# Pooled attention and two feed-forward networks: the start of the kernel is put in another order

## The chip, the core and the metric

The kernel runs on one core of a Trainium2 chip. The metric is the device time of one execution in microseconds (us), taken as the median of several runs. Five engines work side by side: TensorE (PE, with its weight loads PEld), VectorE (DVE), ScalarE (ACT), GpSimd (POOL) and SyncE (SP), whose queue (SPq) issues the transfers (DMAs). Each engine runs its own list of instructions strictly in order.

## What is computed

```
k_p, v_p = mean of k, v over groups of 8 rows             # 8 images, 8 heads, 576 x 64 each
attn = softmax(q @ k_p.T / 8)                             # 576 x 72 for each head
x    = concat over heads of attn @ v_p                    # 4608 tokens x 512
y    = leaky_relu(x @ w_in) @ w_out                       # 512 -> 2048 -> 512
out  = (silu(n @ w_gate) * (n @ w_val)) @ w_out2          # n = RMS norm of y; 512 -> 1536 -> 512
```

All in float32. The kernel makes each large product from two parts of a number, a high part (fp32r) and a low part (the rest), as three matmuls.

## The kernel before

**Stages.** First comes the attention of image 0, then the first network over nine tiles of 512 tokens (j = 0 to 8) with the attention of the other images in between, then the second network. The change lies in the start: the attention of image 0 and the conversion of w_in and w_out, which arrive raw and have to be turned into high and low parts before TensorE can use them.

**Attention of image 0** is a list of steps, named by kind: `kp` (k summed over 8 rows, one DVE reduction of a 128x512 tile, L239), `kt` (k transposed on PE, copied by ACT to kblk, L295), `t` (q transposed), `vp` (`v_prep`, L248), `s` (scores on PE at L325; on DVE maxima L331, subtraction L332; the exponential on ACT L336; on DVE sums L337, L338, reciprocal L339, multiplication L340), `x` (exponentials transposed on PE at L369 and L374, split into parts by ACT and DVE, L371 to L379), `av` (the product with v on PE at L395 and L400, split to the tile `xhl` that the first network reads). Tokens 0 to 255 of the image are the query tiles t = 0, 1 and end in four `av0` steps; the rest, t = 2 to 4 and four `av1` steps, is a list of 13 steps called `second`.

`v_prep` works on six tiles of v: r = 0 to 3 of 128 rows, r = 4 and 5 the "rest" of 96 rows. For image 0 the sum over 8 rows is one DVE reduction (L254); for later images it is `pool_sum` (two additions on GpSimd, L229) and a third addition (L259). Then GpSimd multiplies by a mask (`vm`, L263), ACT takes the high part and DVE the low part (L95, or L270 and L272 for the rest).

**Weights.** `Weights` (W1) holds a list of 36 pieces: w_in and w_out blocks in turn (i0, o0, i1, o1, ...), 28 of them whole (512 KB) and the last 8 in halves. `load` asks for one; `begin` is two instructions on the raw piece, an ACT activation (L139, shown as L98) and a DVE tensor_scalar (L141); `end` is a DVE scalar_tensor_tensor (L149), the high part on ACT and the low part on GpSimd or DVE in turn (both at L95 and L92 in the trace). `step` ends the piece begun, asks for more, and begins the next.

**What sets the order.** The program is traced in the order of the Python code, and a planner with its own model of time then orders each engine's instructions: it may put one that it thinks ready ahead of those traced before it. `tc.keep_in_program_order(x)` ties x behind the instruction traced last before it on its engine, in issue order only. The traced order is `before` (L430 to L443: kp, kt, t, then s0, s1, the six vp, x0, x1, four av0), with one `W1.step` after s1 and one after x1 (L583). Then tile j = 0 runs 24 jobs: f = 0 to 7 on tokens 0 to 255, f = 8 to 15 on all 512, and f = 0 to 7 on tokens 256 to 511. A job f has a `h_unit` (needs w_in block f and xhl), attention slots (the 13 steps of `second` are spread over the first 15 slots, two in a job), the `y_unit` of two jobs earlier (needs w_out of that block and the low part of the activation, DVE L605), and two `W1.step`, three from f = 11 on. The job f = 8 reads all of xhl, so it needs all of `second`.

The transfers of image 0 are asked for in one list (L565 to L574): k, q0, q1, v r = 0 to 4, then i0 and o0, v r = 5 and q2, then i1 and o1, q3, q4, the gain, and four more pieces of weights.

Of the kernel before, what the change touches and what calls it, by code (L numbers as in the profile page):

```python
# [8 lines left out]
F32 = mybir.dt.float32  # L9
# [13 lines left out]
def pooled_attention_then_two_ffns(  # L23
# [13 lines left out]
    nc = tc.nc  # L37
    B, H, S, D = q.shape
    NT, DM = out.shape
    P = 128  # L40
    POOL = 8
    SP = S // POOL
    NP = H // 2
# [45 lines left out]
    def split(hi_eng, hi, lo_eng, lo, src):  # L89

        if hi_eng is nc.scalar:
            nc.scalar.activation(out=hi, in_=src, func=AF.Copy)  # L92
        else:
            hi_eng.tensor_copy(out=hi, in_=src)
        lo_eng.tensor_tensor(out=lo, in0=src, in1=hi.bitcast(F32), op=ALU.subtract)  # L95

    def prelu(out, in_, alpha, scale=1.0):
        return nc.scalar.activation(out=out, in_=in_, func=AF.Prelu, scale=scale, alpha=alpha)  # L98
# [8 lines left out]
    class Weights:  # L107
# [25 lines left out]
        def begin(self):  # L133
            x = self.loaded.pop(0)
            t = x[2]
            top, low = t[:, :, 1], t[:, :, 0]


            prelu(top.bitcast(F32), top.bitcast(F32), 2.0 ** 32, scale=2.0 ** -112)  # L139

            nc.vector.tensor_scalar(  # L141
                out=low, in0=low.bitcast(U32), scalar1=0.9374 * 2.0 ** -29, scalar2=None, op0=ALU.mult
            )
            self.begun.append(x)

        def end(self):
# [22 lines left out]
    ap = att.__enter__()  # L169
# [55 lines left out]
    def pool_sum(x):  # L225

        n = POOL * D // 2
        while n >= 2 * D:
            nc.gpsimd.tensor_tensor(out=x[:, :n], in0=x[:, :n], in1=x[:, n:2 * n], op=ALU.add)  # L229
            n //= 2  # L230
# [17 lines left out]
    def v_prep(b, r):  # L248
        rest = r >= NP
        n = R3 if rest else P  # L250
        x = vraw.pop((b, r))[0:n]
        vs = ap.tile([P, D], F32, tag="vs", bufs=2, name=f"vs{b}_{r}")[0:n]
        if b == 0:
            nc.vector.tensor_reduce(  # L254
                out=vs, in_=x.rearrange("p (r d) -> p d r", r=POOL), axis=AX.X, op=ALU.add
            )
        else:
            pool_sum(x)
            nc.gpsimd.tensor_tensor(out=vs, in0=x[:, 0:D], in1=x[:, D:2 * D], op=ALU.add)  # L259
        m = mask_rest.rearrange("p q h -> p (q h)") if rest else mask_main  # L260
        c = m.shape[1]
        vm = ap.tile([P, 4, D], F32, tag="vm", bufs=1, name=f"vm{b}_{r}")[0:n, 0:c]
        nc.gpsimd.tensor_tensor(  # L263
            out=vm, in0=vs.unsqueeze(1).to_broadcast([n, c, D]),
            in1=m.unsqueeze(2).to_broadcast([n, c, D]), op=ALU.mult,
        )
        if rest:

            t = ap.tile([R3, 4, D], F32R, tag="vbr", bufs=2, name=f"vb{b}_{r}")
            nc.scalar.activation(out=t, in_=vm, func=AF.Copy)  # L270
            z = slice(2 * R1, 3 * R1)
            nc.vector.tensor_tensor(out=t[z], in0=vm[z], in1=t[z].bitcast(F32), op=ALU.subtract)  # L272
        else:
            t = ap.tile([P, 2, 2, D], F32R, tag="vb", bufs=4, name=f"vb{b}_{r}")
            split(nc.scalar, t[:, HI], nc.vector, t[:, LO], vm)
        vb[b, r] = t
# [144 lines left out]
    def need(kind, b, t):  # L421
        if b < B and (kind, b, t) not in done:
            done.add((kind, b, t))
            seq.append((kind, b, t))
# [5 lines left out]
    for part, rs in enumerate(((0, 1, 2), (3, 4))):  # L430
        for r in rs:
            need("kp", 0, r)
        need("kt", 0, part)
        need("t", 0, part)
    need("s", 0, 0)
    need("s", 0, 1)
    for r in range(NP + 2):
        need("vp", 0, r)
    need("x", 0, 0)
    need("x", 0, 1)  # L440
# [9 lines left out]
    for i, (b, t) in enumerate(tiles):  # L450
# [20 lines left out]

    emit = {
        "kp": k_prep, "vp": v_prep, "kt": step_kt, "t": step_t, "s": step_s,
        "x": step_x, "av0": lambda b, p: step_av(b, 0, p), "av1": lambda b, p: step_av(b, 1, p),
    }
# [54 lines left out]
    def run_step(x):  # L530
        kind, b, t = x
        if b > 0:
            top_up(1 if W1.left() else 3)
        emit[kind](b, t)
        if b > 0 and kind in use:
            live["q" if kind == "t" else "kv"] -= 1
# [25 lines left out]
    W1 = Weights(todo1, lambda x: (8 if x[0][1] < 6 else 4) if x[1].stop - x[1].start == 512 else 2)  # L562
# [3 lines left out]
    first += [("q", 0, t) for t in range(2)] + [("v", 0, r) for r in range(NP + 2)]  # L566
    first += [("q", 0, t) for t in range(2, 5)]
    for i in range(0, len(first), 2):
        if i in (12, 14):
            W1.load()  # L570
            W1.load()
        t = per.tile([P, 2, 512], F32, tag=f"w{24 + i // 2}", bufs=1, name=f"first{i}")
        for z, (kind, b, r) in enumerate(first[i:i + 2]):
            {"q": load_q, "k": load_k, "v": load_v}[kind](b, r, t[:, z, :])  # L574
# [5 lines left out]
        W1.load()  # L580
    for x in before:
        run_step(x)
        if x[0] in "sx" and x[2] > 0:  # L583
            W1.step()

    gp = {}
# [95 lines left out]
    def side_steps():  # L682
# [28 lines left out]
        def at(step, f):  # L711
            steps.setdefault(step, []).append(f)

        def unit(begin, n, name, out, src, srcs_of, zs):


# [22 lines left out]
            def store(i):  # L739
                for x, d, dst in held[i]:  # L740
                    own(nc.sync.dma_start(out=dst, in_=d.bitcast(F32).rearrange("p a h n -> p a (h n)")))

            at(begin, start)
            at(begin + 5, lambda: convert(held["raw"]))
            if len(zs) == 2:
# [9 lines left out]
        for p in range(NPAIR):  # L755
            for m, src in (("g", w_gate), ("v", w_val)):
                for c in range(2):
                    def srcs(raw, m=m, p=p, c=c):
                        x = raw.bitcast(F32).rearrange("p (k i n) w -> p k i n w", k=2, i=2)
                        y = op_dram[m, p]  # L760
                        return (
                            ((x[:, 0, :, :, 0], y[:, 1, :, c, :]), (x[:, 1, :, :, 0], y[:, 2, :, c, :])),
                            ((x[:, :, 0, :, 1], y[:, 0, :, c, :]), (x[:, 1, 1:2, :, 1], y[:, 3, 0:1, c, :])),
                        )

                    unit(
                        begin, n, f"{m}{p}_{c}", lambda t: t.rearrange("p (k f) w -> p k (f w)", k=2),
                        src[:, p * 2 * W:(p + 1) * 2 * W].rearrange("(k c p) f -> c p k f", k=2, p=P)[c], srcs,
                        ((0, 6), (1, 8)),
                    )  # L770
                    begin += 6
                    n += 1
            for f in (2 * p, 2 * p + 1):
                def srcs(raw, f=f):
                    x = raw.bitcast(F32)[:, :, 1].unsqueeze(1)
                    return (((x, wo_dram[f].rearrange("p h n -> p (h n)").unsqueeze(1)),),)

                unit(
                    begin, n, f"p{f}", lambda t: t.rearrange("p n w -> p (n w)"), rows(w_out2, f), srcs,
                    ((f % 2, 7),),  # L780
                )
                begin += 4
                n += 1
# [478 lines left out]
```

## Time and profile before

| what | us |
|---|---|
| median of 3 runs | 1807.55 (1806.89 to 1810.25) |
| the profiled execution | 1812.26 |
| its span, first to last instruction | 1810.50 |
| PE busy | 1758.0 |
| DVE, ACT, POOL busy | 891.1, 670.4, 551.2 |

The profile is of one execution. "Busy" counts an engine's instructions; where an engine waits, the row gives the idle time before the instruction in brackets and what released it. PEclk is the granted TensorE clock, where 1.00 is 2.4 GHz and 0.50 is 1.2 GHz. PE is busy nearly all of the span; the time in which it isn't lies mostly in the first 130 us.

### The profile page before, as it was taken

To read this page: it belongs to the slowest core of one execution; us is meant where nothing else is said; L and a number is where in the kernel's file an instruction comes from. 1 tells how busy PE (TensorE), PEld (TensorE's weight loads), DVE (VectorE), ACT (ScalarE), POOL (GpSimd) and SP (SyncE) were. 2 spreads that over 40 slices of the span, in tenths; PEclk is the share of its full clock that TensorE was granted. 3 is DMA by queue.
4 is the path that set the end of the run, shared out by engine and by line. 5 is a ranking of instruction groups with operands and counts; after the bars stand their busy time and mean duration, and the time that the engine had idled before them with its cause. 6 is when DMAs were issued, how large, how long until landed. Compare 5 with 4: busy or idle time off the path is not lost.

```text
span 1810.5 us, 23634 instructions
## 1 busy us (share of the span) xinstructions
PE 1758.0 (97%) x8596; PEld 1498.0 (83%) x8596; DVE 891.1 (49%) x1603; ACT 670.4 (37%) x1424; POOL 551.2 (30%) x681
## 2 busy tenths in 40 slices
PE   3899999999999999999999999999999999999999
PEld 2889887878888888888888888899788889978887
DVE  7974435454356555455344345345534444553331
ACT  5754333443344444344343332243232323322220
POOL 2653303334125142211110442154144204413320
PEclk6999999999999999999999999999999999999999
DMA  8833204447365555435451766687775668776562
GB/s 253 307 109 89 55 21 143 157 140 230 101 189 157 163 157 162 145 125 180 157 172 45 234 195 211 228 300 245 255 245 196 193 226 314 245 250 224 186 209 93
DMA packets 175555, 330.81 MB, mean 183 GB/s; under 512 B 54352, under 2 KB 90192, under 8 KB 174928
## 3 DMA queue, kind: packets, MB, share of 16 engines
q1 hardware_dynamic: 175440, 329.31, 56.1%
q8 instruction: 68, 1.11, 0.3%
q14 instruction: 47, 0.39, 0.1%
HBM read 277.87 MB, written 51.38 MB: 182 GB/s over the span
## 4 chain that ended last, share of the span: by engine, by line
PE 89%; DVE 5%; DMA 3%; issue 1%; ACT 1%; SPq 1%; POOL 1%; ACTq 0%; DVEq 0%; POOLq 0%
PE y L628 20%; PE h L592 20%; PE o L1089 16%; PE yg L1014 6%; PE yv L1014 6%; PE xv L1014 4%; PE xg L1014 4%; PE wg L1014 4%; PE wv L1014 4%; PE sc L325 2%; PE av L395 1%; PE xt L369 1%; DMA wo<-wo 1%; PE qt L303 1%; DMA y<-ye 1%
## 5 line engine op out<-in xcount | busy, mean ns | idle before, releaser
L592 PE MATMUL h<-xhl,w_i 128*128 128x512 f32 (+1 forms) x1824 | 438.2, 385 | 3.1 <-ACT xhl L92 1.3
L592 PEld LDWEIGHTS h<-xhl,w_i 128*128 128x128 f32 x1824 | 329.5, 191 | 68.3 <-DVE xhl L95 4.1
L1089 PE MATMUL o<-wo,u 128*128 128x512 f32 x1296 | 315.1, 390 | 3.5 <-DMA wo<-wo 3.4
L628 PE MATMUL y<-ghl,w_o 128*128 128x512 f32 (+1 forms) x1296 | 285.1, 365 | 1.4 <-DVE ghl L605 1.4
L1089 PEld LDWEIGHTS o<-wo,u 128*128 128x128 f32 x1296 | 242.0, 188 | 53.0 <-DMA wo<-wo 4.9
L628 PEld LDWEIGHTS y<-ghl,w_o 128*128 128x128 f32 x1296 | 218.9, 191 | 35.1 <-DVE ghl L605 1.8
L605 DVE TENSOR_TENSOR ghl<-g,ghl 128x512 fp32r<-128x512 f32 (+1 forms) x152 | 114.6, 754 | 241.5 <-ACT g L98 238.3
L98 ACT ACTIVATE ghl<-h 128x512 fp32r<-128x512 f32 (+1 forms) x152 | 87.0, 572 | 233.4 <-PE h L592 232.9
L628 PE MATMUL y<-ghl,wr 128*128 128x512 f32 x624 | 158.9, 395 | 0.0
L628 PEld LDWEIGHTS y<-ghl,wr 128*128 128x128 f32 x624 | 115.1, 188 | 22.4
L95 POOL TENSOR_TENSOR u<-e2g,u 128x512 fp32r<-128x512 f32 (+1 forms) x25 | 29.7, 1190 | 308.3 <-ACT u L92 308.3
L229 POOL TENSOR_TENSOR v<-v 128x256 f32<-128x256 f32 (+2 forms) x84 | 59.7, 713 | 107.6 <-DMA v<-in_v_dram 105.0
L98 ACT ACTIVATE g<-h 128x512 f32<-128x512 f32 (+1 forms) x152 | 86.8, 571 | 1.0 <-DVE ghl L605 1.0
L1014 PE MATMUL yg<-T,ag 128*128 128x512 f32 (+1 forms) x360 | 84.0, 368 | 0.0
L1014 PE MATMUL yv<-T,av 128*128 128x512 f32 (+1 forms) x360 | 83.8, 368 | 0.0
L1014 PE MATMUL xg<-xa,ag 128*128 128x512 f32 (+1 forms) x360 | 83.8, 367 | 0.0
L1014 PE MATMUL xv<-xa,av 128*128 128x512 f32 (+1 forms) x360 | 83.7, 367 | 0.0
L1014 PEld LDWEIGHTS yg<-T,ag 128*128 128x128 f32 x360 | 66.0, 188 | 10.0 <-DVE e1v L991 0.6
L1014 PEld LDWEIGHTS yv<-T,av 128*128 128x128 f32 x360 | 66.2, 188 | 9.5
L1014 PEld LDWEIGHTS xv<-xa,av 128*128 128x128 f32 x360 | 66.0, 188 | 9.6
L1014 PEld LDWEIGHTS xg<-xa,ag 128*128 128x128 f32 x360 | 66.1, 188 | 9.4
L735 POOL TENSOR_TENSOR parts_g<-raw_g,parts_g 128x256 fp32r<-128x256 f32 (+1 forms) x48 | 33.7, 727 | 102.7 <-ACT parts_g L731 102.7
(166 smaller groups left out, 2596.2 us busy)
## 6 DMA issues: line engine op xcount, KB each, us to landing
wo<-wo SPq DMA_DIRECT2D x120, 512.0 KB
av<-op_v SPq DMA_DIRECT2D x90, 512.0 KB
ag<-op_g SPq DMA_DIRECT2D x90, 512.0 KB
wr<-wo SPq DMA_DIRECT2D x52, 512.0 KB
y<-ye SPq DMA_DIRECT2D x36, 256.0 KB
op_g<-parts_g SPq DMA_DIRECT2D x36, 256.0 KB
op_v<-parts_v SPq DMA_DIRECT2D x36, 256.0 KB
out_dram<-oe SPq DMA_DIRECT2D x36, 256.0 KB
```

Source lines behind the costliest of these rows:

```text
L95: lo_eng.tensor_tensor(out=lo, in0=src, in1=hi.bitcast(F32), op=ALU.subtract)
L98: return nc.scalar.activation(out=out, in_=in_, func=AF.Prelu, scale=scale, alpha=alpha)
L229: nc.gpsimd.tensor_tensor(out=x[:, :n], in0=x[:, :n], in1=x[:, n:2 * n], op=ALU.add)
L303: nc.tensor.transpose(pt[:, c * P:(c + 1) * P], x[:, c * P:(c + 1) * P], ident)
L325: nc.tensor.matmul(pt[:, i * n:(i + 1) * n], y[:, p, :], kblk[b % 2][:, p * n:(p + 1) * n], start=True, stop=True,)
L369: nc.tensor.transpose(pt[:, c * P:(c + 1) * P], e[:, c, 0:P], ident)
L592: nc.tensor.matmul(pt, w[:, sp, c * P:(c + 1) * P], x[:, mp, c, :], start=c == 0 and i == 0, stop=c == n_k - 1 and i == 2,)
L605: nc.vector.tensor_tensor(out=t[:, LO, :], in0=g, in1=t[:, HI, :].bitcast(F32), op=ALU.subtract)
L628: nc.tensor.matmul(pt, w[:, sp, m * P:(m + 1) * P], g[:, mp, a - c0:a - c0 + n], start=ydone[j, a] == 1 and i == 0 and m % per_bank == 0, ...
L735: own(nc.gpsimd.tensor_tensor(out=d[:, :, LO, :], in0=x, in1=d[:, :, HI, :].bitcast(F32), op=ALU.subtract))
L1014: nc.tensor.matmul(pt, wt[:, a, c, sp, :], xt[:, mp, :], start=start and c == 0 and i == 0, stop=c == 1 and i == 2, skip_group_check=not s ...
L1089: nc.tensor.matmul(pt, u[:, sp, m * P:(m + 1) * P], w[:, mp, :], start=f == 0 and i == 0, stop=f == F2 - 1 and i == 2,)
```

## The change

It ties both instructions of `begin` behind the instruction traced before them on their engine, moves the vp steps around the softmax (r = 0, 1 before s0, r = 2 between s0 and s1, the rest after s1), ties the DVE reductions of r = 0 to 3 the same way, gives the sums of r = 4 and 5 to GpSimd, doubles the buffers of vs and vm, asks for i0 and o0 behind all of v and q2, and takes seven W1 steps instead of two in the first part (after s1, x0, x1 and each av0).

```diff
@@ class Weights, begin
-            prelu(top.bitcast(F32), top.bitcast(F32), 2.0 ** 32, scale=2.0 ** -112)
-
-            nc.vector.tensor_scalar(
+            x1 = prelu(top.bitcast(F32), top.bitcast(F32), 2.0 ** 32, scale=2.0 ** -112)
+
+            x2 = nc.vector.tensor_scalar(
                 out=low, in0=low.bitcast(U32), scalar1=0.9374 * 2.0 ** -29, scalar2=None, op0=ALU.mult
             )
+
+            tc.keep_in_program_order(x1)
+            tc.keep_in_program_order(x2)
@@ v_prep
-        vs = ap.tile([P, D], F32, tag="vs", bufs=2, name=f"vs{b}_{r}")[0:n]
-        if b == 0:
-            nc.vector.tensor_reduce(
+        vs = ap.tile([P, D], F32, tag="vs", bufs=4, name=f"vs{b}_{r}")[0:n]
+        if b == 0 and not rest:
+            tc.keep_in_program_order(nc.vector.tensor_reduce(
                 out=vs, in_=x.rearrange("p (r d) -> p d r", r=POOL), axis=AX.X, op=ALU.add
-            )
+            ))
         else:
             pool_sum(x)
             nc.gpsimd.tensor_tensor(out=vs, in0=x[:, 0:D], in1=x[:, D:2 * D], op=ALU.add)
...
-        vm = ap.tile([P, 4, D], F32, tag="vm", bufs=1, name=f"vm{b}_{r}")[0:n, 0:c]
+        vm = ap.tile([P, 4, D], F32, tag="vm", bufs=2, name=f"vm{b}_{r}")[0:n, 0:c]
@@ the order of the steps
+    for r in range(2):
+        need("vp", 0, r)
     need("s", 0, 0)
+    need("vp", 0, 2)
     need("s", 0, 1)
-    for r in range(NP + 2):
+    for r in range(3, NP + 2):
         need("vp", 0, r)
@@ the first transfers
     for i in range(0, len(first), 2):
-        if i in (12, 14):
-            W1.load()
-            W1.load()
+        if i == 14:
+            for _ in range(4):
+                W1.load()
@@ the first part
     for x in before:
         run_step(x)
-        if x[0] in "sx" and x[2] > 0:
+        if x[0] in ("x", "av0") or x[0] == "s" and x[2] > 0:
             W1.step()
```

## Rows read from the trace of the kernel before

**Rows 1.** The page, busy time, share and instructions of each engine.
```profile
PE 1758.0 (97%) x8596; PEld 1498.0 (83%) x8596; DVE 891.1 (49%) x1603; ACT 670.4 (37%) x1424; POOL 551.2 (30%) x681
```
**Rows 2.** Stretches: length, busy time of each engine, PEclk, DMA share, GB/s.
```profile
0.00:39.10 39.10, 11.05 (x42) 7.86 (x42) 30.00 (x55) 19.50 (x50) 9.94 (x25) 0.71 0.81 244
0.00:87.35 87.35, 52.91 (x333) 47.45 (x333) 77.69 (x143) 54.06 (x135) 36.86 (x57) 0.80 0.86 281
39.10:87.35 48.25, 41.86 (x292) 39.58 (x292) 47.68 (x89) 34.55 (x86) 26.92 (x33) 0.88 0.91 311
```
**Rows 3.** PE in order of time: start, us, operation, tiles [idle before].
```profile
39.09 1.01 PE L395 MATMUL av<-at,vb 128*128 128x256 f32 x3 [2.50 <-DVE at L95]
...
87.35 1.94 PE L592 MATMUL h<-xhl,w_i 128*128 128x512 f32 x6 [0.70 <-ACT w_i L92]
```
**Rows 4.** DVE in order of time, 19 to 35 us.
```profile
19.41 0.43 DVE L141 TENSOR_SCALAR raw_i<-raw_i 128x512 int32<-128x512 uint32 x1 [2.48 <-DMA raw_i<-in_moe_w_in_dram]
...
20.73 1.04 DVE L254 TENSOR_REDUCE vs<-first 96x64 f32<-96x512 f32 x1
...
25.51 1.01 DVE L254 TENSOR_REDUCE vs<-first 96x64 f32<-96x512 f32 x1 [0.18 <-POOL vm L263]
26.87 0.43 DVE L141 TENSOR_SCALAR raw_i<-raw_i 128x512 int32<-128x512 uint32 x1 [0.36 <-DMA raw_i<-in_moe_w_in_dram]
...
30.11 0.68 DVE L95 TENSOR_TENSOR w_o<-raw_o,w_o 128x512 fp32r<-128x512 f32 x1
...
34.16 0.76 DVE L340 TENSOR_TENSOR ex<-ex,st 128x576 f32<-128x576 f32 x1
```
**Rows 5.** DVE by line, 0 to 87.35 us: busy, mean ns | idle before.
```profile
L149 DVE SCALAR_TENSOR_TENSOR raw_o<-raw_o 128x512 int32<-128x512 int32 x11 | 9.3, 848 | 0.1
L149 DVE SCALAR_TENSOR_TENSOR raw_i<-raw_i 128x512 int32<-128x512 int32 x11 | 8.8, 804 | 0.1
```
**Rows 6.** One conversion on ACT and DVE, then POOL beside DVE, in order of time.
```profile
19.41 0.68 ACT L98 ACTIVATE raw_i<-raw_i 128x512 f32<-128x512 f32 x1 [4.25 <-DMA raw_i<-in_moe_w_in_dram]
...
20.12 0.69 DVE L149 SCALAR_TENSOR_TENSOR raw_i<-raw_i 128x512 int32<-128x512 int32 x1
...
21.48 0.65 ACT L92 ACTIVATE w_i<-raw_i 128x512 fp32r<-128x512 f32 x1
...
22.21 1.49 POOL L95 TENSOR_TENSOR w_i<-raw_i,w_i 128x512 fp32r<-128x512 f32 x1 [4.80 <-ACT w_i L92]
22.41 0.74 DVE L337 TENSOR_REDUCE st<-ex 128x8 f32<-128x576 f32 x1
...
23.07 0.90 DVE L141 TENSOR_SCALAR raw_o<-raw_o 128x512 int32<-128x512 uint32 x1
```
**Rows 7.** GpSimd's sum of one rest tile of image 1.
```profile
103.25 1.90 POOL L229 TENSOR_TENSOR v<-v 96x256 f32<-96x256 f32 x2
...
105.23 0.39 POOL L259 TENSOR_TENSOR vs<-v 96x64 f32<-96x64 f32 x1
```
**Rows 8.** The SP queue's issues, 11 to 21 us.
```profile
11.33 0.63 SPq L130 DMA_DIRECT2D raw_i<-in_moe_w_in_dram  x1
...
12.59 2.11 SPq L214 DMA_DIRECT2D first<-in_v_dram  x3
...
16.85 4.35 SPq L130 DMA_DIRECT2D raw_i<-in_moe_w_in_dram  x1
```
**Rows 9.** All engines in order of time, 115 to 127 us.
```profile
115.23 0.38 SPq L130 DMA_DIRECT2D raw_o<-in_moe_w_out_dram  x1
...
120.47 0.85 DVE L141 TENSOR_SCALAR raw_o<-raw_o 128x256 int32<-128x256 uint32 x1 [5.11 <-POOL v L229]
...
122.85 1.01 PE L395 MATMUL av<-at,vb 128*128 128x256 f32 x3 [2.71 <-DVE at L95]
```
**Rows 10.** The stretches around that stop, as in rows 2.
```profile
120.00:125.00 5.00, 2.29 (x12) 2.15 (x11) 4.13 (x8) 2.88 (x8) 3.18 (x7) 0.72 0.28 81
125.00:130.00 5.00, 5.00 (x20) 4.46 (x20) 3.76 (x10) 3.55 (x10) 1.59 (x2) 0.59 0.37 129
```

## The prediction

> **What bounds the kernel now.** I read first the busy time of each engine. PE is at work for 1758.0 us of a span of 1810.50 [rows 1], so at most 52.5 us of waiting and some slow clock are to be had, whatever is changed. The second view, the stretches, tells where: up to 87.35 us PE is busy for 52.91, so 34.4 of the 52.5 us lie there [rows 2]. Why the cut at 87.35? PE in order of time shows two marks: the first av at 39.09, behind which the first network begins, and at 87.35 the first one over 512 columns, job f = 8 [rows 3]. That job needs all of image 0's attention; after it PE has whole blocks to work on and hardly waits. I call this mark T8, and price the change by how far T8 moves.
>
> What holds T8 back? In the stretch from 39.10 to 87.35 DVE is busy for 47.68 of 48.25 us [rows 2]: DVE is the bound there and PE, with 41.86, is fed by it. Before 39.10 DVE is busy for 30.00 us only, 9.1 us of waiting. So T8 is 77.69 us of DVE work and 9.7 us of DVE waits [rows 2], and what changes T8 is work taken off DVE ahead of it, or waits of DVE, not PE's early start in itself. The order of DVE's work shows its state best: at 19.41 DVE stands still for 2.48 us, with softmax work behind it, until the first piece of weights has landed, and the multiplication that ends the second softmax is at 34.16 [rows 4]. By T8 11 + 11 pieces have been through `end` [rows 5], while f = 8 needs i0 to i8 and o0 to o7, 17 pieces at most: conversions are ahead of their need, and the attention is late.
>
> **The change part by part.** The sum is made against the profiled execution, 1812.26 us with 1.76 us around its span; that is 4.71 us over the median of the runs, and I take the difference over to the median.
>
> *Two sums to GpSimd.* The two rest reductions on DVE, 1.04 and 1.01 us [rows 4], go: -2.05 us. On GpSimd one such sum takes 1.90 + 0.39 = 2.29 us [rows 7], two take 4.6. GpSimd's busy time in the first 39.1 us is 9.94 [rows 2], so they fit beside it. Who waits for them is the last matmul of an av (L400), 10 us later by the estimate below. Price on DVE: nothing as the near bound, and the 4.6 us as the far one, if DVE stood still for all of it. I take 0, because the DVE work of that stretch is mainly reductions and reads of PSUM, and a reduction of 0.74 us (L337) began inside a GpSimd instruction of 1.49 us and took its usual time; a tensor_scalar in the same place took 0.90 where 0.43 is usual [rows 4, 6].
>
> The Trainium skill ("SBUF — State Buffer", "Who interferes with whom") says that VectorE and GpSimd have one pair of ports under an exclusive lock, that a reduction never takes it, and that a two-input operation in SBUF contends with GpSimd's reads. That speaks against trading a reduction for additions on GpSimd. By it the 4.6 us could be a charge, and the sum would be some 4.6 us dearer; the two rows on L337 and the tensor_scalar agree with it.
>
> *The tie of the conversions.* `begin`'s first DVE instruction now comes behind the multiplication of the second softmax, so the 2.48 us before it and 0.36 at the second one [rows 4] no longer stand ahead of the attention: -2.84 us. Each later `begin` is traced right after an `end`, so it is tied to the piece before it: the pieces become a chain, activation 0.68, L149 0.69, high part 0.65, 2.02 us with nothing between [rows 6], of which DVE works 0.43 + 0.69 and, for each second piece, a low part. Queued behind a tied L141 on DVE are the reduction of v r = 3, and whatever the planner puts there; behind a tied activation on ACT, the exponentials' copies and the parts of av. New DVE waits: at least 0, if attention fills every gap; at most 2.02 - 1.12 = 0.9 for each of the seven pieces of the first part, 6.3 us. I take +1.0, close to the low end, since the 0.57 us of DVE waits in 39.10 to 87.35 [rows 2] show how much work is ready at any time.
>
> *Weights asked for behind v and q2.* On SP the three requests of v r = 5 (2.11 us) pass i0 and o0; i0's request moves from 11.33 to 13.8 at the earliest and, if it meets the pause that the request at 16.85 met, to 16.85 [rows 8]. The first landed 8.1 us after its request, the one of 16.85 by 26.87 [rows 4, 8]. So i0 lands between 21.9 and 26.9. When is DVE there? Of its 30.00 us of work before 39.10 [rows 2] seven L141, six L149 and two low parts are conversions, 7 x 0.43 + 6 x 0.69 + 2 x 0.68 = 8.5 [rows 4, 6], and two reductions go, 2.05: 19.4 us stay, with 9.1 - 2.84 = 6.3 us of waits, 25.7 in all. The first av then comes at 26 to 30 instead of 39.09, an estimate; the second softmax ends some 4 us before it. Cover is thin here, a wait of up to 3 us on i0 is possible, and it is in the +1.0 and its upper bound. vs and vm with more buffers cost nothing: GpSimd waits less, and isn't the bound.
>
> *More steps early.* In traced order the last av1 stands at the end of job 6. By then seven steps of the first part and fourteen of jobs 0 to 6 have begun 21 pieces and ended 20; before the change the planner had let 22 end by T8 [rows 5]. One piece fewer ahead of T8 is 0.43 + 0.69 and half of a low part of 0.68 [rows 4, 6], 1.46 us of DVE. Bounds: 0, if the planner fills as before, and two pieces, -2.9. I take one: -1.46. That work then lies beside jobs of twice the length, where PE is the bound.
>
> *Sum:* -2.05 - 2.84 + 1.0 - 1.46 = -5.35 us for T8. PE idles 5.35 us less, and all after T8 is the same and earlier. 1812.26 - 5.35 = 1806.9 for a profiled execution; 1807.55 - 5.35 = 1802.2 for the median.
>
> *A stop further on that I leave as it is.* At 115.23 a half piece is asked for; DVE and ACT, with its `begin` at the head of their queues, stand still for 5.11 us, PE lives on h and y work, then waits 2.71 for an av of image 1 [rows 9], and the granted clock falls to 0.72 and 0.59 [rows 10], so nearly to the 1.2 GHz level. At 0.59 some 5 us of matmuls cost up to 2 us more, and the same again in the stretch before: I make it 2.71 + 3.1 = 5.8 us, an estimate. The halves now come five steps earlier. Bounds: -5.8, if PE's own work covers the stop, and +2.4, if PE bears all 5.11 us. I take 0, since neither their buffers nor how far ahead they are asked for changes.
>
> **The rivals.** *A: the stop at 115 us goes too.* For: five steps are about two jobs, there PE has no av of image 1 before it. Against: the same two-piece lead and shared buffers. 1802.2 - 5.8 = 1796.4.
>
> *B: the attention is early, T8 isn't.* DVE is the bound to T8, and its work hardly changes; the waits come back as waits of the conversions' chain (the bound 6.3 for the 1.0 taken gives -0.05), or GpSimd's 4.6 us lock DVE out (-0.75). The change would do what it says, the first av at 28, and the time would stay at 1807. For: the first matmul of the network needs i0, i2 lands late. Against: DVE's full queue. This is also what comes out if the planner's other order delivers the same pieces by T8.
>
> *C: the chain of conversions becomes the bound, slower.* f = 8 needs 17 pieces in a row from the first `begin`, about 22.5. At 87.35 - 22.5 = 64.9 us, 3.8 us for each is the point from which T8 comes later than now. Unhindered a piece takes 2.02, and the 22 pieces before T8, overlapped, came each (87.35 - 19.41) / 22 = 3.1 us [rows 3 to 5]. DVE's and ACT's queues add waits to each of three handovers; with 0.65 us at each it is 4.0, T8 17 x 0.2 = 3.4 us late, and the time 1811.0.
>
> **How the numbers follow.** Forecast 0.40; A 0.17; B 0.28; C 0.15. A measurement of this kernel tells 0.2%, 3.6 us, from no change. The forecast's own range, with new waits of 0 to 3 and zero to two pieces, is 1799.8 to 1805.7; some four in five of its cases lie below 1803.9. So faster 0.32 + 0.17 + 0.03 of B = 0.52, same 0.08 + 0.25 = 0.33, slower 0.15. The range of 1796 to 1810 takes in the forecast, A's time and B and leaves out most of C and a stop that is both gone and joined by other gains, 2 in 10.
>
> **What would show each step.** Right: no DVE wait for weights before the last L340 of the second softmax, and that at 20 to 25 instead of 34.16; the first av at 26 to 30; four reductions at L254 and additions at L229 before 25 us; 20 or 21 pieces ended by the first 512-column h; that mark at 82 us. A wait of DVE or ACT on raw_i or raw_o between 22 and 87 that sums to over 4 us shows B; h waiting on w_i, at 3.8 us or more for a piece, shows C; no stop of DVE beyond 2 us past T8 shows A. The forecast is wrong if T8 doesn't move by 2.5 to 8 us, or if it moves and PE's idle time later grows by as much.

## The result, and the profile after

| | kernel before | changed kernel |
|---|---|---|
| median, us | 1807.22 (1806.22 to 1810.25) | 1828.9 (1826.98 to 1830.2, 4 runs) |
| ratio to before | | 1.0116, 95% interval 1.0099 to 1.0134 |
| span of the profiled execution, us | 1810.5 | 1826.8 |

The change makes the kernel 21.7 us slower; 1802.2 was forecast, and 1810 was the end of the range. The page of the changed kernel says where to look: the busy time of each engine, then the chain that ended last.

```profile
PE 1765.4 (97%) x8596; PEld 1501.2 (82%) x8596; DVE 873.1 (48%) x1601; ACT 671.5 (37%) x1424; POOL 543.5 (30%) x687
...
PE 82%; DMA 7%; DVE 4%; POOL 3%; ACT 2%; issue 1%; SPq 1%; POOLq 0%; ACTq 0%; DVEq 0%
```

Against [rows 1] PE is busy 7.4 us longer for the same 8596 matmuls, and not busy for 61.4 us instead of 52.5. So 8.9 of the 16.3 us between the spans are waiting, and 7.4 are busy time that the same matmuls took more. The clock is at most a part of that: 2.6 of the 7.4 lie up to T8 (55.55 us busy, where it was 52.91), and there the granted clock was the higher one, 0.98 against 0.80. From here on 3 is added to most line numbers: L340 of before is L343, L592 is L598, L628 is L634.

**The start moved the forecast way, T8 by about half.** PE in order of time, after:

```profile
29.04 1.01 PE L398 MATMUL av<-at,vb 128*128 128x256 f32 x3 [1.55 <-DVE at L95]
...
84.47 0.73 PE L598 MATMUL h<-xhl,w_i 128*128 128x512 f32 x2 [0.83 <-ACT w_i L92]
```

The first av comes 10.05 us earlier than in [rows 3], the mark T8 2.9 us earlier. The loss is behind it. The stretch from 150 to 200 us, before and then after (columns as in rows 2):

```profile
150.00:200.00 50.00, 49.89 (x336) 45.78 (x335) 27.73 (x58) 20.20 (x56) 20.32 (x39) 1.00 0.31 85
```
```profile
150.00:200.00 50.00, 39.87 (x272) 37.09 (x271) 24.50 (x56) 19.97 (x62) 26.62 (x59) 0.88 0.39 113
```

Before, PE is full here. After, it lacks 10 us and the clock is down to 0.88. These are the marks of the first matmul of some h jobs, worked out from the traces, in us:

| kernel | T8 (f = 8) | f = 9 | f = 10 | f = 11 | f = 13 | last job of tile j = 0 | first job of j = 1 |
|---|---|---|---|---|---|---|---|
| before | 87.3 | 93.2 | 98.2 | 103.3 | 115.6 | 169.3 | 176.9 |
| after | 84.5 | 90.4 | 98.1 | 103.8 | 116.6 | 167.5 | 187.9 |

Two things are to be read off. The lead of 2.9 us is gone by f = 10, before anything went wrong. And the last job of tile j = 0 is no later than before, but j = 1, which needs all of image 1's attention, begins 11 us late. At its third job the lag is 15.5 us, and the first jobs of the later tiles are 13 to 17 us late (17.1 at the last one).

**The first hold: image 1's v stands behind weights on SP.** SP in order of time, after:

```profile
67.67 0.38 SPq L130 DMA_DIRECT2D raw_i<-in_moe_w_in_dram  x1
...
108.03 13.68 SPq L130 DMA_DIRECT2D raw_o<-in_moe_w_out_dram  x2
122.65 0.38 SPq L130 DMA_DIRECT2D raw_i<-in_moe_w_in_dram  x1
124.68 1.98 SPq L217 DMA_DIRECT2D v<-in_v_dram  x3
126.78 0.38 SPq L130 DMA_DIRECT2D raw_i<-in_moe_w_in_dram  x1
128.77 5.17 SPq L130 DMA_DIRECT2D raw_o<-in_moe_w_out_dram  x2
134.58 1.99 SPq L217 DMA_DIRECT2D v<-in_v_dram  x3
136.97 11.84 SPq L206 DMA_DIRECT2D k<-in_k_dram  x5
```

and the same two v tiles before:

```profile
91.83 2.00 SPq L214 DMA_DIRECT2D v<-in_v_dram  x3
...
111.86 1.98 SPq L214 DMA_DIRECT2D v<-in_v_dram  x3
```

The eight half pieces of weights and the k and v tiles of the later images take turns in one set of three buffers (tag raw). SP issues in order: a request whose buffer is not yet free waits, and all behind it wait too. The row of 13.68 us at 108.03 is a whole piece and a half; the half is issued only at 121.37, after a wait of 13.0 us. What it waits for is the first half, asked for at 67.67, whose turn to be converted comes behind all whole pieces (after; ACT, then POOL, which is done with it at 121.34):

```profile
118.44 0.42 ACT L98 ACTIVATE raw_i<-raw_i 128x256 f32<-128x256 f32 x1
...
120.59 0.75 POOL L95 TENSOR_TENSOR w_i<-raw_i,w_i 128x256 fp32r<-128x256 f32 x1 [3.33 <-ACT w_i L92]
```

With five more steps taken early, two halves now stand ahead of v r = 1 to 3 of image 1, five ahead of r = 4 and all eight ahead of r = 5; before, none stood ahead of r = 4 and three ahead of r = 5. So v r = 5 is asked for 22.7 us later. What that delays is a chain that can be followed through four engines (after, in order of time; POOL, ACT, DVE, PE):

```profile
141.91 1.26 POOL L232 TENSOR_TENSOR v<-v 96x256 f32<-96x256 f32 x2 [4.96 <-DMA v<-in_v_dram]
...
145.20 0.61 POOL L266 TENSOR_TENSOR vm<-vs,mask_rest 96x256 f32<-96x256 f32 x1
...
145.84 0.42 ACT L273 ACTIVATE vb<-vm 96x256 fp32r<-96x256 f32 x1 [5.67 <-POOL vm L266]
...
146.29 0.76 DVE L275 TENSOR_TENSOR vb<-vm,vb 32x256 fp32r<-32x256 f32 x1 [5.37 <-ACT vb L273]
...
147.11 0.51 PE L403 MATMUL av<-atr,vb 96*128 96x256 f32 x2 [2.62 <-DVE vb L275]
```

Those are the last two av0 of image 1. The second of them, at 147.3, begins 12.8 us after the request; before it came at 132.5, so it is 14.8 us late. PE waits only 2.62 us here, since it has jobs of j = 0 to do; the bill comes when those have run out. Three query tiles of image 1 and its av1 still have to follow, with little beside them.

**The second hold: the y stores stand behind image 3's k.** ACT, DVE, PE, then the stretch around it, after:

```profile
179.78 0.58 ACT L647 COPY ye<-y 128x512 f32<-128x512 f32 x1 [4.81 <-DMA y<-ye]
180.26 0.69 ACT L339 ACTIVATE ex<-ex 128x576 f32<-128x576 f32 x1
```
```profile
177.26 0.82 DVE L335 TENSOR_TENSOR ex<-sc,st 128x288 f32<-128x288 f32 x2
```
```profile
173.47 0.60 PE L372 MATMUL xt<-ident,ex 128*128 128x128 f32 x4
...
183.57 1.09 PE L372 MATMUL xt<-ident,ex 128*128 128x128 f32 x4 [5.13 <-DVE ex L343]
```
```profile
180.00:190.00 10.00, 5.92 (x20) 5.08 (x21) 4.75 (x12) 4.03 (x13) 6.13 (x15) 0.51 0.65 184
```

A copy of y waits for the store that still reads its buffer, and behind it in ACT's order waits the exponential of image 1's last query tile, for which PE then stands still. What that exponential reads was ready at 178.08 and it began at 180.26, so the copy's wait accounts for 2.2 of PE's 5.13 us; the rest is the softmax of a last tile with nothing beside it. The granted clock was at 0.97 in the ten us ahead of this stretch, in which PE was busy for 6.64 us, and is at 0.51, the 1.2 GHz level, in it: four xt matmuls take 1.09 us here and took 0.60 at 173.47. And why was the store late? SP in order of time, after:

```profile
161.43 10.07 SPq L217 DMA_DIRECT2D v<-in_v_dram  x6
171.60 0.85 SPq L206 DMA_DIRECT2D k<-in_k_dram  x2
...
172.98 1.73 SPq L650 DMA_DIRECT2D y<-ye  x2
```

The first copies of y were done at 170.4, but the stores stand behind image 2's last v, for which SP waits 10 us, and behind the first k of image 3; before, that k stood behind them.

### The profile page after: what moved, and what is told of

It is laid out like the page before. It is cut to its first block, busy times and chain, and to the rows that moved or that the text cites. A ratio compares the mean times of both kernels' runs of the same rounds, so it can differ in the third digit from the quotient of the medians.

```text
span 1826.8 us, 23650 instructions
## 1 busy us (share of the span) xinstructions
PE 1765.4 (97%) x8596; PEld 1501.2 (82%) x8596; DVE 873.1 (48%) x1601; ACT 671.5 (37%) x1424; POOL 543.5 (30%) x687
## 4 chain that ended last, share of the span: by engine, by line
PE 82%; DMA 7%; DVE 4%; POOL 3%; ACT 2%; issue 1%; SPq 1%; POOLq 0%; ACTq 0%; DVEq 0%
PE y L634 17%; PE h L598 17%; PE o L1095 15%; PE yg L1020 6%; PE yv L1020 6%; PE xg L1020 4%; PE xv L1020 4%; PE wv L1020 4%; PE wg L1020 4%; DMA v<-in_v_dram 3%; PE sc L328 2%; POOL v L232 1%; DMA y<-ye 1%; PE av L398 1%; DMA raw_i<-in_moe_w_in_dram 1%
## 5 line engine op out<-in xcount | busy, mean ns | idle before, releaser
L598 PE MATMUL h<-xhl,w_i 128*128 128x512 f32 (+1 forms) x1824 | 442.4, 386 | 9.4 <-ACT w_i L92 5.9
L598 PEld LDWEIGHTS h<-xhl,w_i 128*128 128x128 f32 x1824 | 329.5, 191 | 74.0 <-ACT w_i L92 7.2
L634 PE MATMUL y<-ghl,w_o 128*128 128x512 f32 (+1 forms) x1296 | 286.7, 366 | 3.2 <-ACT ghl L98 2.3
L634 PEld LDWEIGHTS y<-ghl,w_o 128*128 128x128 f32 x1296 | 220.9, 192 | 39.6 <-ACT ghl L98 4.0
L611 DVE TENSOR_TENSOR ghl<-g,ghl 128x512 fp32r<-128x512 f32 (+1 forms) x152 | 107.0, 704 | 236.2 <-ACT g L98 235.8
L634 PE MATMUL y<-ghl,wr 128*128 128x512 f32 x624 | 158.9, 395 | 1.1 <-ACT ghl L98 1.1
L634 PEld LDWEIGHTS y<-ghl,wr 128*128 128x128 f32 x624 | 115.1, 188 | 23.7 <-ACT ghl L98 1.3
```

The source lines that it names most:

```text
L598: nc.tensor.matmul(pt, w[:, sp, c * P:(c + 1) * P], x[:, mp, c, :], start=c == 0 and i == 0, stop=c == n_k - 1 and i == 2,)
L611: nc.vector.tensor_tensor(out=t[:, LO, :], in0=g, in1=t[:, HI, :].bitcast(F32), op=ALU.subtract)
L634: nc.tensor.matmul(pt, w[:, sp, m * P:(m + 1) * P], g[:, mp, a - c0:a - c0 + n], start=ydone[j, a] == 1 and i == 0 and m % per_bank == 0, ...
```

## The experiments

The first theories were *buffers* (the halves hold the raw buffers that image 1's v needs, and their place on SP is the cause) and *chain* (the tied conversions are themselves the bound). The theory *two holds* came after the first eight. Profiles of one kernel scatter: the kernel before and a copy of it with another queue for its stores have equal medians, but 4.1 us lie between the starts of j = 1 in their two profiles, and 1.3 us between their marks T8. A mark is therefore read only where it moves by more, and the ratios carry the verdicts. A ratio of 0.001 is 1.8 us.

**One part taken out of the change.** `old_steps` takes the two W1 steps of before:

```diff
-        if x[0] in ("x", "av0") or x[0] == "s" and x[2] > 0:
+        if x[0] in "sx" and x[2] > 0:
```

> The changed kernel with one part undone: W1.step after s1 and x1 only, as before, so the eight half pieces of weights are asked for behind v r = 4 of image 1 again and not among v r = 1 to 4. Theory (buffers): the halves share three buffers with the later images' k and v; asked for five steps earlier and converted late, they keep v r = 4 and 5 of image 1 waiting (asked for at 124.68 and 134.58 us in the changed kernel, 91.83 and 111.86 before), and TensorE waits for image 1 at the start of the second tile. Then this kernel is back at 1800 to 1808 us, with v r = 4 asked for before 100 us. Rival (chain): the ties make the conversions a chain, and their late end costs the time; then it stays at 1820 us or more.

Measured 1.0057 (1.0037 to 1.0078), 1820.0 us. All halves are again behind v r = 4 on SP, but r = 5 is asked for at 119.97, and image 3's k is still ahead of the y stores. Half of the loss is gone, not all: a miss for *buffers* as the only cause. Here the second hold shows most clearly. The first copies of y are done by 166.4, the store is issued at 174.14, the next copy waits for it, and behind that copy stand the copies of exponentials that PE needs (ACT, then PE):

```profile
177.47 0.58 ACT L647 COPY ye<-y 128x512 f32<-128x512 f32 x1 [6.41 <-DMA y<-ye]
```
```profile
178.27 0.66 PE L377 MATMUL xr<-ident,er 128*96 128x128 f32 x2 [6.11 <-ACT er L366]
```

`no_ties` leaves out the two `keep_in_program_order` in `begin`.

> The changed kernel without the two ties of the conversions; the seven early steps, and with them the order in which the shared buffers are given out, stay as in the changed kernel. Buffers: still slow, 1812 to 1828 us, less by as much as the halves are converted sooner and free their buffers sooner. Chain: back at 1800 to 1808 us.

Measured 1.0059 (1.0039 to 1.0078), 1819.6 us. The halves stand where the change puts them, but without the ties they are converted sooner and free their buffers sooner: v r = 5 is asked for at 126.04 instead of 134.58. So it takes both, requests that are early and conversions that are late, to make the whole hold.

**One part put into the kernel before.** `steps_alone` has only the seven steps, `ties_alone` only the two ties.

> The kernel before with one part of the change alone: seven early W1 steps in place of two. Buffers: slower than before, 1812 to 1828 us, with v r = 4 of image 1 asked for after 105 us. Chain: as before, 1804 to 1810 us.

Measured 1.0013 (1.0001 to 1.0024), 1810.5 us: v r = 4 at 114.83 and r = 5 at 125.70, the y stores ahead of image 3's k. The time is under the 1812 of *buffers*, a miss: in this kernel a v r = 5 that is asked for 13.8 us late costs some 4 us at most (1.0024).

> The kernel before with the ties of the conversions alone. Buffers: 1803 to 1810 us, as the halves stand behind v r = 4 of image 1 as before. Chain: 1818 us or more, as each piece takes 3.2 to 3.5 us after the one before it.

Measured 1.0034 (1.0021 to 1.0047), 1813.6 us, between the two theories and in the range of neither: v r = 5 at 125.21. Neither part alone costs what both cost together.

`bufs_alone` doubles vs and vm in the kernel before:

```diff
-        vs = ap.tile([P, D], F32, tag="vs", bufs=2, ...
+        vs = ap.tile([P, D], F32, tag="vs", bufs=4, ...
-        vm = ap.tile([P, 4, D], F32, tag="vm", bufs=1, ...
+        vm = ap.tile([P, 4, D], F32, tag="vm", bufs=2, ...
```

> The kernel before with one part of the change alone: four buffers for vs and two for vm in place of two and one. Theory (store behind k): with more of them GpSimd's sums of image 2 run ahead, k of image 3 is asked for ahead of the first tile's y stores on SP, the stores wait there for buffers, and ACT's copies of y wait for the stores with the next tile's attention behind them. Then it is slower than before, 1811 to 1819 us, with the first y store issued after k of image 3 and an ACT wait on it of over 3 us at 170 to 185 us. Rival (off the path): GpSimd isn't the bound, so nothing changes, 1804 to 1810 us.

Measured 1.0065 (1.0047 to 1.0083), 1819.0 us. The time is at the upper end of the range, the place is not the expected one. Image 3's k is ahead of the y stores, but no copy of ACT waits for a store, and in the profile the start of j = 1 is late by 4.9 us, and all of that is there at f = 12, before any store. With more buffers the planner ordered the start anew: a rest sum goes ahead of the softmax on DVE and waits there for its transfer (DVE, 17 to 25 us):

```profile
17.36 1.01 DVE L254 TENSOR_REDUCE vs<-first 96x64 f32<-96x512 f32 x1 [2.59 <-DMA first<-in_q_dram]
...
23.97 1.01 DVE L254 TENSOR_REDUCE vs<-first 96x64 f32<-96x512 f32 x1 [2.56 <-DMA first<-in_v_dram]
```

So buffers of which "GpSimd waits less" were not free; that the stores' place made this price is not shown by this run.

**Parts taken out or put together with small buffers.** `small_vs` is the change with vs 2 and vm 1.

> The changed kernel with vs and vm back at two buffers and one. Store behind k: the y stores go ahead of k of image 3, and 5 to 9 us come back, 1819 to 1824 us. Off the path: 1826 to 1831 us. The shared buffers of the halves stay as in the changed kernel, so v r = 5 of image 1 is asked for after 125 us in both cases.

Measured 1.0063 (1.0045 to 1.0081), 1819.8 us. The y stores are ahead of image 3's k again; the first hold is there in full (v r = 5 at 134.30).

`v_small` has only the order of the vp steps with the ties of the four reductions, the two sums on GpSimd and the later weights (two W1 steps, no ties in `begin`, vs 2 and vm 1).

> Only the order of the v steps, the two sums on GpSimd and the later request of the weights; no ties of the conversions, two early steps, vs and vm with the buffers of before. If these three parts are worth what I put down for them (two reductions less on DVE, no wait for weights ahead of the softmax) and nothing downstream is disturbed, 1802 to 1806 us; if the time is set by image 1 at the start of the second tile, 1805 to 1810 us whatever the start of the first does.

Measured 1.0049 (1.0030 to 1.0068), 1817.1 us: a miss. It has neither hold (v r = 5 at 111.81). Without the ties DVE's conversions stand ahead of the softmax as before and now wait longer, since the weights are asked for later (DVE, from 22 us):

```profile
22.14 0.43 DVE L141 TENSOR_SCALAR raw_i<-raw_i 128x512 int32<-128x512 uint32 x1 [3.93 <-DMA raw_i<-in_moe_w_in_dram]
...
31.97 1.84 DVE L341 TENSOR_TENSOR ex<-ex,st 128x576 f32<-128x576 f32 x1
```

[rows 4] has 2.48 us there. That explains about 1.5 us (the mark T8 is 1.6 late, hardly more than profiles scatter); where the rest comes in isn't settled.

`raw4` is `small_vs` with a fourth raw buffer.

> The changed kernel with a fourth buffer for the raw k, v and half pieces (the space comes from vs and vm, back at two and one). Buffers: v r = 5 of image 1 is asked for 10 us sooner or more than in the kernel with three, the last av of its first part comes 12 to 14 us after that, and the time is 8 to 15 us under that of the kernel with vs and vm alone undone, 1808 to 1815 us. Chain: the conversions still end after 130 us, and the time is that of the kernel with vs and vm undone, within 2 us.

Measured 1.0102 (1.0085 to 1.0119), 1826.2 us, 6.3 us worse than without it, a miss for both theories. v r = 4 and 5 are asked for at 123.26 and 133.62, hardly sooner than the 124.87 and 134.30 of `small_vs`: requests are served in order, so a further buffer goes to the next half in the queue. And image 3's k is ahead of the y stores again. So the fourth buffer didn't cure the first hold, and the second one came back; what each is worth here isn't separated.

**The two holds, one by one.** `hold4` has all of the change, and asks for halves only once v r = 4 of image 1 has been asked for:

```diff
+            v_asked.add((b, t))
...
-    W1 = Weights(todo1, lambda x: (8 if x[0][1] < 6 else 4) if x[1].stop - x[1].start == 512 else 2)
+    v_asked = set()
+    W1 = Weights(todo1, lambda x: (8 if x[0][1] < 6 else 4) if x[1].stop - x[1].start == 512
+                 else 2 if (1, 4) in v_asked else 0)
```

`y_other_queue` is the change with the y stores issued from ACT's queue:

```diff
-                nc.sync.dma_start(
+                nc.scalar.dma_start(
```

`hold4_y_other_queue` has both edits, `hold4_small_vs` has the first one with vs 2 and vm 1.

> The changed kernel; the y stores of L650 are issued from ACT's queue instead of SP's, nothing else is altered. Theory 'two holds on SP' (the halves' weight requests hold image 1's v, and k requests of image 3 hold the y stores of tile j=0): only the second hold is taken away, so the 9.1 us that lie between the changed kernel (1828.9) and the one with vs 2 and vm 1 (1819.8) come back: 1817 to 1822, no ye copy of ACT that waits for a y store, and no wait of PE over 2 us for image 1's last tile between 176 and 186 us; tile j=1 still starts at 183 to 188 us. Rival 'the stores are only bystanders' (the planner's other order on DVE, ACT and PE costs it): 1826 to 1831.

> The changed kernel; the eight half weight pieces are asked for only once the request of v r=4 of image 1 has been planned. Theory 'two holds on SP': the first hold is taken away, v r=5 of image 1 is asked for before 115 us (134.58 in the changed kernel), the last av of its first half comes before 135 us (147.3), tile j=1 starts at 175 to 181 us (187.9), and what stays is the hold of the y stores: 1813 to 1821. Rival 'the chain of conversions is itself the bound': the halves come still later, tile j=0 ends over 170 us, and the time is 1826 or more.

> Both edits: halves asked for behind v r=4 of image 1, y stores issued from ACT. Theory 'two holds on SP': both go, and the start's gain of about 3 us is left: 1802 to 1811. Rival 'the chain is the bound' or 'other order of the engines': 1817 or more.

> The changed kernel with vs 2 and vm 1 and with the halves asked for behind v r=4 of image 1; the y stores of tile j=0 are planned ahead of image 3's k on SP again, by the small buffers. Theory 'two holds on SP': both holds are gone in another way, 1803 to 1811, tile j=1 starts at 174 to 180 us (186.1 with the small buffers alone). Rival 'the chain is the bound': 1818 or more, tile j=1 at 183 us or later.

Ratios to the kernel before, with the 95% interval:

| | halves as in the change | halves behind v r = 4 |
|---|---|---|
| vs 4, vm 2, y stores on SP | 1.0116 (1.0099 to 1.0134) | 1.0024 (1.0013 to 1.0035) |
| y stores on ACT | 1.008 (1.006 to 1.010) | 1.0004 (0.9991 to 1.0018) |
| vs 2, vm 1 | 1.0063 (1.0045 to 1.0081) | 1.0000 (0.9989 to 1.0012) |

The times of `hold4`, `hold4_y_other_queue` and `hold4_small_vs` lie in the ranges of *two holds*; `y_other_queue`, 1823.1 us where the kernel before had 1809.1, is 1 us over its range and under that of the rival. Going right in the table, the first hold costs 0.92, 0.76 and 0.63%, that is 16.6, 13.7 and 11.4 us. Going down, the second costs 6.5 us beside the first hold and 3.6 without it by the stores, 9.6 and 4.3 by the buffers. These differences of two ratios are uncertain by 0.15 to 0.3%, so the first hold is certain, and the second is clear of zero by little, with 3.6 and 4.3 us least.

The profiles say less of the second hold than the ratios. With the stores on ACT the changed kernel's first store is issued at 168.49 instead of 172.98, but the second only at 174.75 instead of 173.60: ACT itself stands for 5.10 us around it and for 2.67 us later, and j = 1 begins at 189.87, not in the 183 to 188 expected. This profiled execution, 1825.66 us, was one of the two longer ones of four (1820.2 to 1825.7), so where the 6.5 us of the runs come back isn't shown. And in `hold4` image 3's k is still ahead of the stores, yet the first goes out at 172.27, 0.8 us behind its copy, and PE is busy for 34.95 of the 35 us from 165 to 200: in that profile the second hold costs nothing.

With both holds gone the kernel is where it was before. In `hold4` v r = 5 is asked for at 118.64 (a miss, before 115 was expected), the last av0 of image 1 comes at 131.4 and j = 1 begins at 177.0. PE in the stretch in which the change lost its time, `hold4_y_other_queue`:

```profile
165.00:200.00 35.00, 35.00 (x211) 30.95 (x210) 19.88 (x45) 14.88 (x39) 16.83 (x34) 1.00 0.35 105
```

and the changed kernel:

```profile
165.00:200.00 35.00, 24.87 (x154) 22.09 (x153) 17.61 (x42) 13.46 (x40) 17.62 (x39) 0.85 0.39 115
```

**Controls, and what the terms are worth once the queue is in order.** `before_y_other_queue` is the kernel before with its y stores on ACT. `hold4_small_y` has all three cures (vs 2 and vm 1, halves behind v r = 4, stores on ACT). `hold4_y_no_ties` is `hold4_y_other_queue` without the ties; `hold4_old_steps` is `hold4_small_vs` with the steps of before.

> The kernel before with the y stores issued from ACT's queue and nothing else altered: a control for that edit. Theory: in the kernel before the y stores of tile j=0 stand ahead of image 3's k on SP and hold nobody, so the edit is worth nothing there: 1805 to 1810. Rival 'ACT's queue is a better place whatever stands on SP': 1803 or less.

Measured 0.9998 (0.9986 to 1.0010): ACT's queue is worth nothing by itself, so the 6.5 us are not the worth of a better queue. The Trainium skill ("DMA: Bandwidth & Descriptors", "Issuing engines are not separate DMA queues") says that issuing from another engine saves only the time that the issue takes. The kernel before agrees; in the changed kernel the 6.5 us are more than an issue on ACT takes (0.4 us), for which the stand of SP ahead of the stores is the likely reason, not shown by the profile.

> All three edits: vs 2 and vm 1, halves behind v r=4 of image 1, y stores from ACT. Theory: either of the last two ways of freeing the stores is enough, so this is the same as each alone, 1804 to 1811. Rival 'the start's gain of 3 us shows once every hold is gone': 1802 to 1804.

Measured 0.9995 (0.9986 to 1.0005), 1807.6 us: the same as before, as the theory said. The lead at the start doesn't show at the end.

> Both holds taken away (halves behind v r=4 of image 1, y stores from ACT) and the two ties taken out; everything else of the changed kernel stays. Tells what the ties are worth in the start once the queue is in order. Theory 'the ties bring the attention forward and the conversions pay it back': first av 6 us or more later than the 29 us with ties, f=8 within 2 us of the 84.8 us with ties, time within 0.2% of that kernel, 1805 to 1812. Rival 'the serial chain of conversions costs what the start gains' (no ties are better): 1800 to 1804. Rival of the prediction, 'the ties are the gain': f=8 at 87 us or later, 1811 to 1815.

Measured 1.0033 (1.0020 to 1.0046) against 1.0004 with the ties, 1814.1 us: the theory's range is missed. The first av is at 38.15 instead of about 29 and T8 at 89.5 instead of 84.8, so the ties do carry the start, as the rival said. But at the start of j = 1 only 0.8 us are left of the 4.7 (177.3 and 176.5), and in these two profiles the rest appears between tiles j = 3 and 4. There the same 446 matmuls took 98.50 us of PE and not 96.01, at a granted clock of 0.97 and not 1.00: most of this rest is a slow clock in one of the profiles, and why the ratio of nine runs is 1.0033 stays open.

> vs 2, vm 1, halves behind v r=4 of image 1 and the old condition of the weight steps: of the seven earlier conversion steps none is left. Theory 'the early steps only matter through the queue': f=8 later by 0 to 3 us than with them, the time within 0.2%, 1805 to 1812. Rival 'the early steps are what the start needs with the ties' : f=8 at 88 us or later, 1812 to 1818.

Measured 1.0010 (0.9995 to 1.0026); T8 at 86.3, v r = 5 at 121.99. By the theory: the early steps are worth nothing that can be measured, and their harm was their place on the queue.

Buffers of their own for the halves, which would end the sharing altogether, were not tried.

## Why the prediction was wrong

**Reading the start: right.** There is no wait for weights ahead of the second softmax's last multiplication, which is at 25.08 instead of 34.16 [rows 4], at the edge of the 20 to 25 given, and the first av at 29.04 lies in the forecast 26 to 30. The first piece, asked for later, is begun at 22.07, near the early end of 21.9 to 26.9, and holds nobody up.

**Two sums to GpSimd: right, but the collision came elsewhere.** GpSimd's additions for both took 2.9 us, not 4.6. Beside them a reduction took its usual 0.74 us, and beside the mask's multiplication a tensor_scalar 0.62 instead of 0.43 (POOL, then DVE, after):

```profile
20.31 1.54 POOL L232 TENSOR_TENSOR first<-first 96x256 f32<-96x256 f32 x3 [3.47 <-DMA first<-in_v_dram]
20.54 0.74 DVE L340 TENSOR_REDUCE st<-ex 128x8 f32<-128x576 f32 x1
...
27.27 0.72 POOL L266 TENSOR_TENSOR vm<-vs,mask_main 128x128 f32<-128x128 f32 x1 [4.50 <-DVE vs L257]
27.65 0.62 DVE L141 TENSOR_SCALAR raw_o<-raw_o 128x512 int32<-128x512 uint32 x1
```

The charge of up to 4.6 us that the Trainium skill's rule on the shared ports ("SBUF — State Buffer", "Who interferes with whom") allowed did not come for these sums; what came was in line with it. A charge that I had not thought of came with the ties: in the chain, L152 of a w_out block falls beside GpSimd's low part of the w_in block before it, and took 1.26 us in the mean, where that of a w_in block took 0.72 and before both took 0.80 to 0.85 [rows 5] (DVE by line up to T8, after):

```profile
L152 DVE SCALAR_TENSOR_TENSOR raw_o<-raw_o 128x512 int32<-128x512 int32 x8 | 10.1, 1259 | 1.5 <-ACT raw_o L98 1.3
L152 DVE SCALAR_TENSOR_TENSOR raw_i<-raw_i 128x512 int32<-128x512 int32 x9 | 6.5, 722 | 0.1
```

**The sum for T8: -5.35 forecast, -2.9 measured; two terms were mis-sized and partly cancel.** To T8 DVE did 70.03 us of work and waited 14.4, where it was 77.69 and 9.7 [rows 2]. The work fell by 7.7 and not by 3.5, since at T8 only 17 pieces have been through `end`, the least that f = 8 needs, where I took 20 or 21: five pieces fewer than before, not one. With the two sums that would be 9.4 us less by the prediction's prices; the collision at L152 took back some of it. The waits rose by 4.8 instead of falling by 1.84: beside the 2.84 that went, 7.6 new ones came, for the +1.0 taken, and more than the bound of 6.3. The stretch, then where the chain waits (ACT by line from 21 to 120 us: busy, mean ns | idle before):

```profile
0.00:84.47 84.47, 55.55 (x331) 48.26 (x331) 70.03 (x136) 50.59 (x132) 35.37 (x61) 0.98 0.87 277
```
```profile
L92 ACT ACTIVATE w_i<-raw_i 128x512 fp32r<-128x512 f32 x14 | 9.5, 680 | 9.2 <-DVE raw_i L152 9.2
L92 ACT ACTIVATE w_o<-raw_o 128x512 fp32r<-128x512 f32 x14 | 9.4, 673 | 8.4 <-DVE raw_o L152 8.4
```

From the first to the last whole piece, 22.07 to 115.77 us, a piece takes 93.7 / 27 = 3.47 us, under the 3.8 at which rival C would have made T8 late. C was right in kind: T8 waits for its own w_i, 0.83 us. Past T8 the jobs come nearly at the chain's pace (next paragraph).

**"All after T8 is the same and earlier": wrong, for two reasons.** First, each job behind T8 needs two more pieces, 6.9 us at the chain's pace, and the jobs f = 8 to 13 of before came every 5.7 us (28.3 / 5). With no stock of converted pieces left, the jobs come every 6.4 us (32.1 / 5), near the chain's pace, and the lead is used up by f = 10. I had called the pieces "ahead of their need" and booked one piece fewer as a gain; the surplus was what the jobs after T8 lived on. The four kernels with the ties and without the holds have T8 at 82.6 to 86.3 us, f = 10 at 97.2 to 100.5 (98.2 and 96.8 in the two profiles of before), and the time of before, to 0.1%. Second, the price by one mark left out every request that stands further down the same queue. This was the larger error, nearly all of the loss: 1.0116 falls to 1.0004 when only the queue is put in order.

**"Neither their buffers nor how far ahead they are asked for changes": wrong.** Both numbers are indeed the same. But five steps earlier in the traced order means that the halves' requests are traced ahead of image 1's v, and later conversions mean that they hold their shared buffers longer. The stop at 115 us did go, as rival A had it, and gave nothing: f = 13 is no earlier, SP stands longer, and DVE stops later, for 2.77 us at 132 and 5.37 us at 146. A's price was a little high besides: in the slow stretch before, PE was busy for 2.29 us at 0.72 [rows 10], which costs some 0.6 us and not 1.1.

**"vs and vm with more buffers cost nothing": wrong.** On the changed kernel they cost 9.6 us (1.0116 against 1.0063), and on the kernel before 1.0065. I looked at who would wait less, and not at what would then be asked for sooner. In the profiles of the changed kernel the k requests move up on SP with them, and the stores fall behind requests that must wait; on the kernel before the loss is in the start, in the planner's other order.

**The rivals and the range.** No rival named a request that waits further down the queue. C's price was its only slower end, 1811, and the time lies 18 us beyond it.

## What to carry to other kernels

Before moving a request, list what stands behind it on its queue and whose buffer it waits for: a request that waits for a buffer holds every load and store behind it. A buffer that is shared in turn by two streams makes the order of requests part of the critical path, and a further buffer goes to whichever stream is next in that order. And a mark that moves earlier is a gain only if what feeds the work after it comes as fast as that work; work that seems ahead of its need may be the stock that the next stage lives on.

## What had not been expected of the hardware

The matmuls behind a pause of PE were slow too. In the changed kernel PE waited for 5.13 us and was then busy for 5.92 us of the 10 from 180 to 190 us, at a granted clock of 0.51, where the kernel before ran at 1.00. By the two xt rows, 1.09 and 0.60 us, those 5.92 us would have been some 3.3 at the 2.4 GHz level, an estimate; so about 2.7 of the 7.4 us by which the same 8596 matmuls took longer. The rest is not explained: 2.6 of it lie ahead of T8, at a higher clock than before.

A chain in a fixed order can make two engines meet at every turn. L152 of the w_out blocks took 1.26 us in the mean beside GpSimd's low part of w_in; 0.69 is what the same instruction took at 20.12 us in the kernel before [rows 6].
